# Converted weights: sign by a leaky slope on ScalarE, first loads on one queue, two maxima by GpSimd's queue

## The chip, the cores and the metric

One core of one Trainium2 chip. The metric is the device time of one execution in microseconds (us); lower is better. Before the change three runs gave a median of 1084.42 us (1084.20 to 1084.54).

## What is computed

A windowed attention whose weights are a softmax over seven taps, followed by a SiLU MLP. Cut from the reference (`x`: 4 x 4096 x 192, eight heads of 24 columns, `w_in`: 192 x 2048, `w_out`: 2048 x 192):

```python
w = softmax(weight_gen, axis=-1)                      # (B, S, 8 heads, 7 taps)
out[b, s, h, :] = sum_k w[b, s, h, k] * x_pad[b, s + k, h, :]   # window of 7, padded in front
h = out.reshape(16384, 192) @ w_in
result = (h * sigmoid(h)) @ w_out                     # (16384, 192), float32
```

`x` and `weight_gen` come as float32, `w_in` and `w_out` as float64. The chip gets each float64 as two 32-bit integers, low and high, and makes float32 of them itself.

## The kernel before, in words

**Tiling.** The 16384 rows lie 128 to a partition. They are worked in 32 blocks `b` of 512 rows (four per partition), each against 16 slices `f` of 128 hidden columns, taken as 8 pairs `p` (slices `p` and `p + 8`). For each pair (`b`, `p`) TensorE does `mm1` (the hidden columns, L497 for block 0, L509 from block 1), ScalarE the SiLU (`act`, L519 or L521 and L522), VectorE the low half of a two-part float16 split (`lower`, L527, from block 1), and TensorE the second product (`mm2_whole`, L550 and L554, or `mm2`, L541). Block 0 runs in float32 on the converted weights as they are. From block 1 on everything is split in two float16 parts, which needs a power of two as scale: one for each weight matrix, one for each chunk of `x`. Chunk 1 is block 1, chunk 2 is blocks 2 and 3, and the later chunks have four blocks each. `mm1` runs three pairs ahead of the second product, with four PSUM tiles for `h`, so two pairs of `h` can be open.

**Opening.** The engines' orders are written out by hand up to the end of block 1. First come the loads; then the softmax of block 0 (`top`, `sub`, `exp`, `tot`, `rec`, `norm`: L318 to L337); then seven products of `x` with a tap's weight on VectorE (L450), which TensorE sums in PSUM through an identity matrix (`total`, L455; the last two products are added on VectorE first, L460); copies to SBUF (L465, L466); a turn by TensorE (L471) with copies (L472); then `mm1` of block 0 (L497). 64 small matmuls at the start (L619) warm TensorE up.

**Weights.** Eight pieces of each matrix, `I0` to `I7` and `O0` to `O7`, are loaded as raw integers into nine buffers by SP's queue (L193, L196). Each piece is converted (`convert_steps`): `move` on ScalarE (L211) scales the high word, read as a float32, by 2^-112; `sign` on VectorE shifts the low word right (L173) and puts the high word's sign bit over it (L216); `join` (L220) shifts the moved value left by three and merges. `size` on ScalarE (L225) sums the absolute values of a piece, and of these sums the scale comes: `w_rows` (L254) on VectorE, a turn on TensorE (L257), a maximum on VectorE (L260), a spread over the partitions on TensorE (L264), and the scale on VectorE (`w_scale`). Then each piece is split (`upper_w` L238, `lower_w` L242).

**Scales of x.** For chunk 1 ScalarE sums absolute values (L640, `xs1`), TensorE turns the column into a row (L647), VectorE takes the maximum (L660), TensorE spreads it (L661). For chunk 2 (L666, `xs2`) and the later chunks the column goes by DMA to DRAM and back, spread over all partitions (`absmax_by_dma`, L160 and L161), on SP's queue.

**Order.** `OPENING` has a row for each of the first 16 pairs, with three strings of step names: before the pair's `mm1`, after its `act`, and inside the second product that follows. `I S J B U L` with a digit are move, sign, join, size, upper and lower of a piece of `w_in`; `O G Q D P R` the same of `w_out`; `n1`, `n2` the rest of the softmax of chunks 1 and 2; `M`, `A` products and sums of block 1's attention; `X` its split and transposes (L393, L396, L403, L388); `Wr Wa Wb Wc` the steps of the weight scale; `y` chunk 1's scale; `x2` the size of chunk 2 and its DMAs; `z2` chunk 2's scale from them; `g` the lower part of the pair before. Every engine and queue works in its order; a step that waits holds all behind it.

The lines that the diff touches, with those that call them:

Of the kernel before, what the change touches and what calls it, by code (L numbers as in the profile page):

```python
# [62 lines left out]
REBIAS = 2.0 ** -112  # L63
RAW = 9
SIGN = -0x80000000
# [4 lines left out]
def kernel(  # L70
# [132 lines left out]
    wsum = const.tile([P, 2, NP], F32, name="wsum")  # L203

    def convert_steps(kind, p):

        v, t = value(kind, p), stage.tile([P, 2 * D], I32, tag="t", name=f"t{kind}{p}", bufs=2)
        col = "IO".index(kind)

        def move():  # L210
            nc.scalar.activation(out=v, in_=raws[kind, p][..., 1].bitcast(F32), func=AF.Copy, scale=REBIAS)  # L211

        def sign():
            low, high = raws[kind, p][..., 0], raws[kind, p][..., 1]
# [8 lines left out]
        def size():
            junk = sm_p.tile([P, 2 * D], mybir.dt.bfloat16, tag="junk", name=f"junk{kind}{p}", bufs=1)
            nc.scalar.activation(out=junk, in_=v, func=AF.Abs, accum_out=wsum[:, col, p:p + 1])  # L225

        return [move, sign, join, size]
# [46 lines left out]
    def load_x(c):  # L274
# [4 lines left out]
        if t0 == 0:  # L279
# [5 lines left out]
            nc.scalar.dma_start(out=t[1:1 + cut, 0:HALO, :], in_=xf[0:cut, T - HALO:T, :])  # L285
            nc.scalar.dma_start(out=t[1 + cut:P, 0:HALO, :], in_=xf[cut:P - 1, T - HALO:T, :])
# [312 lines left out]
    with tc.manual_schedule():  # L599
        load_w(0)  # L600
        load_x(0)
        load_w(1, nc.scalar)
        load_w(2, nc.scalar)
# [5 lines left out]
        load_x(1)  # L609
        load_piece("I", 1)  # L610
# [19 lines left out]
        for f in (top1, sub1, exp1, step.pop("zeros"), top2, sub2, exp2):  # L630
            f()
        nc.scalar.activation(out=warm[:, 1:2], in_=ones[0:1, 0:1], func=AF.Silu)
        for k in range(5, 1, -1):
            mul(k)
            total(k, False, False)
        xs1 = sm_p.tile([P, 1], F32, tag="xs1", name="xs1", bufs=1)
        xs2 = sm_p.tile([P, 1], F32, tag="xs2", name="xs2", bufs=1)
        rows1 = (HALO + TB) * D
# [6 lines left out]
        px = ps_o.tile([P, 2, D], F32, tag="acc", name="x1_all").rearrange("p a d -> p (a d)")  # L645
        pw = ps_o.tile([P, 2, D], F32, tag="acc", name="w_all").rearrange("p a d -> p (a d)")
        nc.tensor.matmul(px[0:1, 0:P], xs1, ident, start=True, stop=True)  # L647
        total(1, False, True)

        conv = {(k, p): convert_steps(k, p) for k in "IO" for p in range(NP)}  # L650
        conv["I", 0][0]()
# [7 lines left out]
        x1r = sm_p.tile([1, 1], F32, tag="r", name="r_x1")  # L659
        nc.vector.tensor_reduce(out=x1r, in_=px[0:1, 0:P], op=ALU.max, axis=AX.X)  # L660
        nc.tensor.matmul(px[:, P:P + 1], ones[0:1], x1r, start=True, stop=True)  # L661

        def x2_size():
            n = (HALO + chunks[2][1]) * D
            junk = xv.rearrange("p t g n -> p (t g n)").bitcast(mybir.dt.bfloat16)[:, 0:n]
            nc.scalar.activation(out=junk, in_=x_t[2][:, 0:HALO + chunks[2][1], :].rearrange("p t d -> p (t d)"),  # L666
                                 func=AF.Abs, accum_out=xs2)
            got, (rows, over) = absmax_by_dma(xs2, "x2")
            rows()
            step["z2"] = lambda: (over(), x_scales(got, 2), finish_scales(2), out_scale(2))  # L670
# [149 lines left out]
```

## Time and profile before

| | |
|---|---|
| median of three runs | 1084.42 us |
| the profiled execution | 1084.3 us, of which its span is 1082.5 us |
| TensorE (PE) busy | 1049.9 us, 97% of the span |
| VectorE (DVE) busy | 784.7 us, 72% |
| ScalarE (ACT) busy | 775.0 us, 72% |
| GpSimd (POOL) busy | 293.2 us, 27% |
| DMA queue of SP / of ACT | 64.43 MB / 0.93 MB |

The span is what the profiler's records cover; 1.8 us lie around it. PE is the engine whose order fills the span; what it does not fill lies almost all in the first 100 us. Rows of the timeline give the start of a group of like instructions, the time to the end of its last one, the engine and line, output and input, shapes, and the count; in brackets stands the time that the engine sat idle before, and what ended it. SPq and ACTq are the issues of those engines' DMA queues.

### The profile page before, as it was taken

To read this page: it belongs to the slowest core of one execution; us is meant where nothing else is said; L and a number is where in the kernel's file an instruction comes from. 1 tells how busy PE (TensorE), PEld (TensorE's weight loads), DVE (VectorE), ACT (ScalarE), POOL (GpSimd) and SP (SyncE) were. 2 spreads that over 40 slices of the span, in tenths; PEclk is the share of its full clock that TensorE was granted. 3 is DMA by queue.
4 is the path that set the end of the run, shared out by engine and by line. 5 is a ranking of instruction groups with operands and counts; after the bars stand their busy time and mean duration, and the time that the engine had idled before them with its cause. 6 is when DMAs were issued, how large, how long until landed. Compare 5 with 4: busy or idle time off the path is not lost.

```text
span 1082.5 us, 36860 instructions
## 1 busy us (share of the span) xinstructions
PE 1049.9 (97%) x16472; PEld 811.3 (75%) x16472; DVE 784.7 (72%) x1134; ACT 775.0 (72%) x1264; POOL 293.2 (27%) x169
## 2 busy tenths in 40 slices
PE   6988999999999999999999998999999999999998
PEld 4655677777777777777777776777777777777776
DVE  6888886678866697677867686667886669767643
ACT  3765777678777777777767785767877777777775
POOL 1000343331513343312433304333151334331100
PEclk9999999999999999999999999999999999999999
DMA  8412132111411115111331104111131111211110
GB/s 214 139 30 118 42 133 50 39 45 32 131 46 45 39 38 145 32 31 46 91 85 46 46 19 142 39 39 46 31 131 46 45 38 40 48 31 32 45 46 16
DMA packets 73790, 67.71 MB, mean 63 GB/s; under 512 B 52639, under 2 KB 67103, under 8 KB 72606
## 3 DMA queue, kind: packets, MB, share of 16 engines
q1 hardware_dynamic: 73184, 64.43, 21.8%
q8 instruction: 128, 2.10, 0.9%
q10 hardware_dynamic: 446, 0.93, 0.3%
q14 instruction: 32, 0.26, 0.1%
HBM read 28.37 MB, written 12.59 MB: 38 GB/s over the span
## 4 chain that ended last, share of the span: by engine, by line
PE 77%; DVE 9%; ACT 6%; DMA 5%; issue 3%; SPq 0%; DVEq 0%; ACTq 0%
PE h L509 37%; PE acc L541 37%; DVE pr L424 2%; ACT h L521 2%; DVE g L527 1%; PE acc L554 1%; DVE pr L418 1%; DMA xc<-in_x_dram 1%; DMA xu<-xt 1%; DMA xt<-xs 1%; DVE xm L351 1%; ACT g L522 1%; DMA d_x<-xs 1%; PE sum L455 1%; PE h L497 1%
## 5 line engine op out<-in xcount | busy, mean ns | idle before, releaser
L527 DVE SCALAR_TENSOR_TENSOR g<-h,gup,g 128x512 f16<-128x512 f32 x496 | 369.0, 747 | 264.8 <-ACT g L522 264.4
L541 PE MATMUL acc<-wo,g 64*128 64x192 f16 x11424 | 556.6, 243 | 0.0
L541 PEld LDWEIGHTS <-g 64*128 64x128 f16 x11424 | 528.5, 94 | 25.2 <-issue 0.2
L521 ACT ACTIVATE h<-h,inv 128x512 f32<-128x512 f32 x496 | 326.5, 658 | 251.0 <-PE h L509 250.2
L509 PEld LDWEIGHTS <-w 64*128 64x128 f16 x4464 | 278.7, 94 | 203.4 <-issue 24.0
L522 ACT ACTIVATE g<-h,gup 128x512 f16<-128x512 f32 x496 | 341.0, 687 | 16.2
L509 PE MATMUL h<-xt,w 64*128 64x512 f16 x2232 | 310.7, 376 | 10.8 <-DVE g L527 10.8
L509 PE MATMUL h<-xu,w 64*128 64x512 f16 x2232 | 308.8, 377 | 4.3 <-DMA xu<-xt 4.3
L418 POOL TENSOR_TENSOR pr<-xc,wc 128x768 f32<-128x768 f32 x87 | 144.4, 1674 | 507.5 <-DVE pr L424 407.2
L418 DVE TENSOR_TENSOR pr<-xc,wc 128x768 f32<-128x768 f32 x130 | 130.9, 1008 | 0.0
L424 DVE TENSOR_TENSOR pr<-pr,pr 128x768 f32<-128x768 f32 x128 | 130.1, 1016 | 0.3
L424 POOL TENSOR_TENSOR pr<-pr,pr 128x768 f32<-128x768 f32 x58 | 122.2, 2107 | 4.5
L575 DVE SCALAR_TENSOR_TENSOR o<-acc,od,t 128x192 f32<-128x192 f32 x120 | 44.1, 408 | 3.5 <-ACT t L574 3.5
L574 ACT ACTIVATE t<-acc,od 128x192 f32<-128x192 f32 x120 | 43.6, 418 | 3.8 <-PE acc L554 3.8
L321 POOL TENSOR_TENSOR wc<-wc,wm 128x896 f32<-128x896 f32 x7 | 12.3, 1757 | 107.6 <-DVE wm L318 107.6
L396 DVE SCALAR_TENSOR_TENSOR xs<-pr,xup,xs 128x768 f16<-128x768 f32 x31 | 35.3, 1138 | 6.4 <-ACT xs L393 4.3
L337 POOL TENSOR_TENSOR wc<-wc,ws 128x896 f32<-128x896 f32 x7 | 12.3, 1754 | 89.6 <-DVE ws L334 89.6
L393 ACT ACTIVATE xs<-pr,xup 128x768 f16<-128x768 f32 x31 | 28.7, 925 | 9.1 <-DVE pr L424 9.1
L351 DVE TENSOR_REDUCE xm<-xc 128x1 f32<-128x960 f32 (+1 forms) x28 | 34.4, 1228 | 0.0
L550 PEld LDWEIGHTS acc<-v_out,g 128*128 128x128 f32 x128 | 21.4, 196 | 4.9 <-issue 1.8
L550 PE MATMUL acc<-v_out,g 128*128 128x192 f32 x128 | 24.3, 344 | 0.0
L554 PEld LDWEIGHTS <-g 128*128 128x128 f16 x240 | 20.1, 100 | 5.4 <-issue 5.1
(87 smaller groups left out, 254.6 us busy)
## 6 DMA issues: line engine op xcount, KB each, us to landing
xc<-in_x_dram SPq DMA_DIRECT2D x7, 2112.0 KB, 10.4
xu<-xt SPq DMA_DIRECT2D x62, 192.0 KB, 2.8
out_dram<-o SPq DMA_DIRECT2D x58, 192.0 KB, 1.9
wc<-in_weight_gen_dram SPq DMA_DIRECT2D x7, 448.0 KB, 6.4
rawI<-in_moe_w_in_dram SPq DMA_DIRECT2D x16, 192.0 KB, 6.5
rawO<-in_moe_w_out_dram SPq DMA_DIRECT2D x8, 384.0 KB, 4.3
xc<-in_x_dram SPq DMA_DIRECT2D x1, 1344.0 KB
xc<-in_x_dram SPq DMA_DIRECT2D x2, 384.0 KB, 6.0
```

The source lines that it names most:

```text
L351: nc.vector.tensor_reduce(out=m[:, i:i + 1], in_=x_t[c][:, cuts[i]:cuts[i + 1], :].rearrange("p t d -> p (t d)"), op=ALU.max, axis=AX.X, a ...
L396: nc.vector.scalar_tensor_tensor(out=xs[:, ts, D:2 * D], in0=acc, scalar=sc[c, "up"], in1=xs[:, ts, 0:D], op0=ALU.mult, op1=ALU.subtract)
L418: eng.tensor_tensor(out=pr[k].rearrange("p t (h g) -> p (t h) g", g=G), in0=xin, in1=wv, op=ALU.mult)
L424: eng.tensor_tensor(out=pr[k], in0=pr[k], in1=pr[l], op=ALU.add)
L509: nc.tensor.matmul(h_t[b, p + NP * i], w16[rows, g, part, p * P:(p + 1) * P], x_in[rows, :, k, :], start=n == 0, stop=n == NT9 - 1)
L521: nc.scalar.activation(out=h, in_=h, func=AF.Silu, scale=sc[c, "inv"])
L522: nc.scalar.activation(out=gh, in_=h, func=AF.Copy, scale=sc[c, "gup"])
L527: nc.vector.scalar_tensor_tensor(out=gl_t[b, f], in0=h, scalar=sc[chunk_of[b], "gup"], in1=gh_t[b, f], op0=ALU.mult, op1=ALU.subtract)
L541: nc.tensor.matmul(acc_t[b, i, t // 2][:, t % 2, :], g[rows, t * P:(t + 1) * P], wo16[rows, f, part], start=f == ORDER[0] and t % 2 == 0 a ...
L550: nc.tensor.matmul(acc_t[b, 0, t // 2][:, t % 2, :], gh_t[b, f][:, t * P:(t + 1) * P], v_out[:, f % NP, f // NP], start=f == 0 and t % 2 = ...
L574: nc.scalar.activation(out=t1, in_=a[0], func=AF.Copy, scale=sc[c, "od"])
L575: nc.vector.scalar_tensor_tensor(out=o[:, t, :], in0=a[1], scalar=sc[c, "od"], in1=t1, op0=ALU.mult, op1=ALU.add)
```

## The change

Five things are edited. `move` uses a leaky function: a positive value is scaled by 2^-112 as before, a negative one also by -2^32, which sets the bit that `join` shifts into the sign, so the merge of the sign bit on VectorE (L216) is gone and `rest` is the shift alone. `size` takes two pieces at once. The halo rows of `x` and the softmax weights of chunks 1 and 2 are loaded on SP's queue, where ACT's queue had them. The maxima of chunks 1 and 2 go through DRAM on GpSimd's queue; chunk 1's no longer passes TensorE. The order of the opening is written anew: the softmax starts of chunks 1 and 2 stand between products of block 0, and in `OPENING` six of `M` and `A` are ahead of `Wr`, `Wa` is half a second product later, and `z2` three pairs later.

```diff
-    ("", "D6 D7 Wr M3 A3", "Wa M2 A2"),
-    ("Wb M1 A1 M0 A0 X", "Wc U0 L0 U1 U2 P0 L1", "L2 U3 R0 P1 L3"),
+    ("", "D3 M1 A1 Wr M0 A0 X", ""),
+    ("Wa", "Wb", "Wc U0 U1 P0 L0 L1"),
...
-    wsum = const.tile([P, 2, NP], F32, name="wsum")
+    wsum = const.tile([P, 2, NP // 2], F32, name="wsum")
...
         def move():
-            nc.scalar.activation(out=v, in_=raws[kind, p][..., 1].bitcast(F32), func=AF.Copy, scale=REBIAS)
-
-        def sign():
-            low, high = raws[kind, p][..., 0], raws[kind, p][..., 1]
-            bits(t, low, 29, ALU.logical_shift_right)
-            nc.vector.scalar_tensor_tensor(out=t, in0=high, scalar=SIGN, in1=t,
-                                           op0=ALU.bitwise_and, op1=ALU.bitwise_or)
+            nc.scalar.activation(out=v, in_=raws[kind, p][..., 1].bitcast(F32), func=AF.Prelu, scale=REBIAS,
+                                 alpha=TO_BIT_31)
+
+        def rest():
+            bits(t, raws[kind, p][..., 0], 29, ALU.logical_shift_right)
...
-            nc.scalar.dma_start(out=t[1:1 + cut, 0:HALO, :], in_=xf[0:cut, T - HALO:T, :])
-            nc.scalar.dma_start(out=t[1 + cut:P, 0:HALO, :], in_=xf[cut:P - 1, T - HALO:T, :])
+            nc.sync.dma_start(out=t[1:1 + cut, 0:HALO, :], in_=xf[0:cut, T - HALO:T, :])
+            nc.sync.dma_start(out=t[1 + cut:P, 0:HALO, :], in_=xf[cut:P - 1, T - HALO:T, :])
...
-        load_w(1, nc.scalar)
-        load_w(2, nc.scalar)
+        load_w(1)
...
         load_x(1)
+        load_w(2)
...
-        for f in (top1, sub1, exp1, step.pop("zeros"), top2, sub2, exp2):
-            f()
-        nc.scalar.activation(out=warm[:, 1:2], in_=ones[0:1, 0:1], func=AF.Silu)
+        step.pop("zeros")()
+        between = {5: (top1, sub1, exp1), 4: (top2, sub2, exp2)}
         for k in range(5, 1, -1):
             mul(k)
             total(k, False, False)
+            for f in between.get(k, ()):
+                f()
+        nc.scalar.activation(out=warm[:, 1:2], in_=ones[0:1, 0:1], func=AF.Silu)
...
-        px = ps_o.tile([P, 2, D], F32, tag="acc", name="x1_all").rearrange("p a d -> p (a d)")
+        got1, (to_all1, over1) = absmax_by_dma(xs1, "x1", nc.gpsimd)
+        to_all1()
...
-        nc.tensor.matmul(px[0:1, 0:P], xs1, ident, start=True, stop=True)
+        spare = ps_o.tile([P, 2, D], F32, tag="acc", name="spare").rearrange("p a d -> p (a d)")
+        nc.tensor.matmul(spare[:, 0:P], ident16, ident16, start=True, stop=True)
...
-        x1r = sm_p.tile([1, 1], F32, tag="r", name="r_x1")
-        nc.vector.tensor_reduce(out=x1r, in_=px[0:1, 0:P], op=ALU.max, axis=AX.X)
-        nc.tensor.matmul(px[:, P:P + 1], ones[0:1], x1r, start=True, stop=True)
...
-            got, (rows, over) = absmax_by_dma(xs2, "x2")
+            got, (rows, over) = absmax_by_dma(xs2, "x2", nc.gpsimd)
```

**SP's queue, the first loads.** `wc` are the softmax weights, `xc` the rows of `x`, `raw` the pieces of the weights. Before:

```order
L307 DMA wc_112<-in_weight_gen_dram 128x224
L284 DMA xc_114<-in_x_dram 128x768
L193 DMA rawI_133<-in_moe_w_in_dram 64x3x256 x2
L299 DMA xc_114<-in_x_dram 128x768
L193 DMA rawI_137<-in_moe_w_in_dram 64x3x256 x2
```

After:

```order
L308 DMA wc_112<-in_weight_gen_dram 128x224
L285 DMA xc_114<-in_x_dram 128x768
L286 DMA xc_114<-in_x_dram 112x1152
L287 DMA xc_114<-in_x_dram 15x1152
L308 DMA wc_119<-in_weight_gen_dram 128x224
L193 DMA rawI_131<-in_moe_w_in_dram 64x3x256 x2
L300 DMA xc_114<-in_x_dram 128x768
L308 DMA wc_135<-in_weight_gen_dram 128x448
```

The two halo loads and both later softmax weights, four issues that stood first on ACT, now stand among SP's, and the first raw piece is behind them.

**VectorE, from the last pieces of the weights to the weight scale.** `pr` are products of block 1's attention (the first line number of a pair a product, the second a sum), `tI` and `tO` the scratch of a conversion. Before:

```order
L418 TENSOR_TENSOR pr_1_351<-xc_114,wc_119 128x768
L424 TENSOR_TENSOR pr_0_350<-pr_0_350,pr_1_351 128x768
L173 TENSOR_SCALAR tI_304<-rawI_165 128x384
L216 SCALAR_TENSOR_TENSOR tI_304<-rawI_165,tI_304 128x384
L220 SCALAR_TENSOR_TENSOR v_in<-v_in,tI_304 128x384
L173 TENSOR_SCALAR tO_311<-rawO_170 128x384
L216 SCALAR_TENSOR_TENSOR tO_311<-rawO_170,tO_311 128x384
L220 SCALAR_TENSOR_TENSOR v_out<-v_out,tO_311 128x384
...
L418 TENSOR_TENSOR pr_2_352<-xc_114,wc_119 128x768
L424 TENSOR_TENSOR pr_0_350<-pr_0_350,pr_2_352 128x768
L254 TENSOR_REDUCE w_rows<-wsum 128x2
```

After:

```order
L419 TENSOR_TENSOR pr_3_353<-xc_114,wc_119 128x768
L425 TENSOR_TENSOR pr_0_350<-pr_0_350,pr_3_353 128x768
L173 TENSOR_SCALAR tI_295<-rawI_165 128x384
L218 SCALAR_TENSOR_TENSOR v_in<-v_in,tI_295 128x384
L173 TENSOR_SCALAR tO_302<-rawO_170 128x384
L218 SCALAR_TENSOR_TENSOR v_out<-v_out,tO_302 128x384
...
L419 TENSOR_TENSOR pr_4_354<-xc_114,wc_119 128x768
L425 TENSOR_TENSOR pr_0_350<-pr_0_350,pr_4_354 128x768
L419 TENSOR_TENSOR pr_5_355<-xc_114,wc_119 128x768
L425 TENSOR_TENSOR pr_0_350<-pr_0_350,pr_5_355 128x768
L255 TENSOR_REDUCE w_rows<-wsum 128x2
```

A piece takes two instructions where it took three, and ahead of the reduction stand six products and five sums where three and two stood.

**GpSimd, its first work after the identity matrices.** `d_x` is the column in DRAM, `mb_x` its copy over all partitions. After (before, the memset was followed at once by the first product):

```order
L292 MEMSET xc_114 1x1152
L160 DMA d_x_309<-xs_286 128x1
L161 DMA mb_x_310<-d_x_309 128x128
L160 DMA d_x_660<-xs_287 128x1
L161 DMA mb_x_661<-d_x_660 128x128
L419 TENSOR_TENSOR pr_0_640<-xc_389,wc_135 128x768
```

Four DMAs stand ahead of the first product of block 3, each waiting for the size or the DMA before it.

## Rows read from the trace of the kernel before

**Rows 1.** The page: span, and busy time of TensorE with its weight loads.

```profile
span 1082.5 us, 36860 instructions
PE 1049.9 (97%) x16472; PEld 811.3 (75%) x16472; DVE 784.7 (72%) x1134; ACT 775.0 (72%) x1264; POOL 293.2 (27%) x169
```

**Rows 2.** Timeline of TensorE, sums of block 0 to block 1.

```profile
22.23 1.56 PE L455 MATMUL sum<-pr,ident 128*128 128x384 f32 x4
...
26.20 0.38 PE L661 MATMUL x_all<-r_x,ones 1*128 1x1 f32 x2 [0.84 <-DVE r_x L660]
26.51 8.01 PE L497 MATMUL h<-xv,v_in 64*128 64x256 f32 x48
34.45 2.87 PE L550 MATMUL acc<-v_out,g 128*128 128x192 f32 x16
...
56.34 0.38 PE L257 MATMUL w_all<-ident,w_rows 128*2 128x128 f32 x2 [3.60 <-DVE w_rows L254]
...
73.56 1.24 PE L509 MATMUL h<-xu,w 64*128 64x512 f16 x9 [1.07 <-DMA xu<-xt]
...
89.35 0.37 PE L509 MATMUL h<-xt,w 64*128 64x512 f16 x1 [2.60 <-DVE g L527]
```

**Rows 3.** Three stretches: busy time by engine, granted clock, DMA share, GB/s.

```profile
15.00:22.00 7.00, 7.00 (x17) 3.72 (x18) 6.50 (x9) 3.28 (x5) 0.00 (x0) 0.76 1.12 269
56.30:62.90 6.60, 6.56 (x25) 3.90 (x25) 6.46 (x9) 0.00 (x0) 0.00 (x0) 0.74 0.00 0
86.80:97.80 11.00, 8.17 (x61) 4.57 (x60) 10.22 (x19) 3.97 (x7) 0.00 (x0) 0.84 0.62 260
```

**Rows 4.** Timeline of all engines, loads to the last product of block 0.

```profile
5.48 0.39 DVE L318 TENSOR_REDUCE wm<-wc 128x32 f32<-128x224 f32 x1 [4.49 <-DMA wc<-in_weight_gen_dram]
...
6.26 1.28 ACT L623 ACT_TABLE_LOAD   x1 [6.26 <-DMA xc<-in_x_dram]
...
7.66 0.37 ACT L325 ACTIVATE wc<-wc 128x224 f32<-128x224 f32 x1
...
9.51 0.96 DVE L450 TENSOR_TENSOR pr<-xc,wc 128x768 f32<-128x768 f32 x1
...
19.19 0.96 DVE L460 TENSOR_TENSOR pr<-pr,pr 128x768 f32<-128x768 f32 x1
```

**Rows 5.** Timeline of VectorE, conversions to the weight scale.

```profile
26.07 0.34 DVE L173 TENSOR_SCALAR tI<-rawI 128x384 int32<-128x384 int32 x1
...
30.95 0.56 DVE L220 SCALAR_TENSOR_TENSOR v_out<-v_out,tO 128x384 int32<-128x384 int32 x1 [0.89 <-ACT v_out L211]
...
47.96 0.95 DVE L418 TENSOR_TENSOR pr<-xc,wc 128x768 f32<-128x768 f32 x1
...
49.82 0.35 DVE L173 TENSOR_SCALAR tI<-rawI 128x384 int32<-128x384 int32 x1
50.21 0.56 DVE L216 SCALAR_TENSOR_TENSOR tI<-rawI,tI 128x384 int32<-128x384 int32 x1
50.87 0.56 DVE L220 SCALAR_TENSOR_TENSOR v_in<-v_in,tI 128x384 int32<-128x384 int32 x1
...
51.34 0.35 DVE L173 TENSOR_SCALAR tO<-rawO 128x384 int32<-128x384 int32 x1
...
56.12 0.16 DVE L254 TENSOR_REDUCE w_rows<-wsum 128x2 f32<-128x16 f32 x1
```

**Rows 6.** Timeline of VectorE, block 1: split, chunk 2's scale, next lower pair.

```profile
65.16 1.02 DVE L396 SCALAR_TENSOR_TENSOR xs<-pr,xup,xs 128x768 f16<-128x768 f32 x1 [1.00 <-ACT xs L393]
...
87.41 0.28 DVE L166 TENSOR_REDUCE ra_x<-mb_x 128x1 f32<-128x128 f32 x1 [1.11 <-DMA mb_x<-d_x]
...
88.56 1.40 DVE L527 SCALAR_TENSOR_TENSOR g<-h,gup,g 128x512 f16<-128x512 f32 x2
```

**Rows 7.** The DMAs through DRAM (column out, and back), issue to landing.

```profile
DMA to landing us min/median/max: 4.0/5.1/9.0
```

**Rows 8.** Waits of TensorE over the whole span: total us, times, longest.

```profile
PE h L509 <- DMA xu<-xt: 4.3, 3, 2.8
```

More of the change, by code (lines that the diff above doesn't have):

```diff
@@ L63 @@
 REBIAS = 2.0 ** -112
+TO_BIT_31 = -2.0 ** 32
 RAW = 9
-SIGN = -0x80000000
 EXPONENT = 0x7F800000
@@ L221, in join, with size_w @@
                                            op0=ALU.logical_shift_left, op1=ALU.bitwise_or)
[L223 to L227, printed above, removed]
+        return [move, rest, join]
+    def size_w(kind, q):
+        v = v_in if kind == "I" else v_out
+        v = v[:, 2 * q:2 * q + 2].rearrange("p q a n -> p (q a n)")
+        col = "IO".index(kind)
+        junk = sm_p.tile([P, 4 * D], mybir.dt.bfloat16, tag="junk", name=f"junk{kind}{q}", bufs=1)
+        nc.scalar.activation(out=junk, in_=v, func=AF.Abs, accum_out=wsum[:, col, q:q + 1])
     def halves_of(kind, p):
@@ L635 @@
             total(k, False, False)
+            for f in between.get(k, ()):
+                f()
+        nc.scalar.activation(out=warm[:, 1:2], in_=ones[0:1, 0:1], func=AF.Silu)
         xs1 = sm_p.tile([P, 1], F32, tag="xs1", name="xs1", bufs=1)
         xs2 = sm_p.tile([P, 1], F32, tag="xs2", name="xs2", bufs=1)
+        conv = {(k, p): convert_steps(k, p) for k in "IO" for p in range(NP)}
+        conv["I", 0][0]()
         rows1 = (HALO + TB) * D
@@ L644 @@
         both(1, 0)
-        px = ps_o.tile([P, 2, D], F32, tag="acc", name="x1_all").rearrange("p a d -> p (a d)")
+        got1, (to_all1, over1) = absmax_by_dma(xs1, "x1", nc.gpsimd)
+        to_all1()
         pw = ps_o.tile([P, 2, D], F32, tag="acc", name="w_all").rearrange("p a d -> p (a d)")
-        nc.tensor.matmul(px[0:1, 0:P], xs1, ident, start=True, stop=True)
+        spare = ps_o.tile([P, 2, D], F32, tag="acc", name="spare").rearrange("p a d -> p (a d)")
+        nc.tensor.matmul(spare[:, 0:P], ident16, ident16, start=True, stop=True)
         total(1, False, True)
-        conv = {(k, p): convert_steps(k, p) for k in "IO" for p in range(NP)}
-        conv["I", 0][0]()
         conv["I", 0][1]()
@@ L677, in w_scale @@
             out_scale(1)
-        step |= {"y": lambda: x_scales({"all": px[:, P:P + 1]}, 1), "x2": x2_size, "n2": lambda: (tot2(), rec2(), norm2()), "n1": lambda: (tot1(), rec1(), norm1()),
+        step |= {"y": lambda: (over1(), x_scales(got1, 1)), "x2": x2_size, "n2": lambda: (tot2(), rec2(), norm2()), "n1": lambda: (tot1(), rec1(), norm1()),
                  "Wr": w_rows, "Wa": w_turn, "Wb": w_over, "Wc": w_scale}
         for p in range(NP):
-            for kind, names in (("I", "ISJ" "B" "UL"), ("O", "OGQ" "D" "PR")):
+            for kind, names in (("I", "ISJUL"), ("O", "OGQPR")):
                 steps = conv[kind, p] + [lambda k=kind, p=p: upper_w(k, p), lambda k=kind, p=p: lower_w(k, p)]
                 step.update({f"{n}{p}": f for n, f in zip(names, steps)})
+                if p % 2 == 0:
+                    step["BD"["IO".index(kind)] + str(p // 2)] = lambda k=kind, p=p: size_w(k, p // 2)
         for n in ("I0", "S0", "J0"):
```

18 rows, old and new, of the table OPENING are left out of this document.

## The prediction

> **What bounds the kernel now.** I read the page first: TensorE is busy for 97% of the span [rows 1], so a microsecond counts only where TensorE's own order moves. Then the timeline of TensorE [rows 2]: the reader is to look for the brackets. Up to 26.51 us it does little but sum block 0; from there its order is nearly closed, but for four gaps: 3.60 us for the weight scale's row sums, 1.07 for the swapped rows, 2.60 for a lower part on VectorE, and 0.84 for the maximum that stands ahead of the first `mm1`. Then the granted clock [rows 3]: its mean is 0.76, 0.74 and 0.84 over three stretches. As the clock has two levels, 1.2 and 2.4 GHz, the time at the lower is twice the missing share: 7.0 x 0.24 x 2 = 3.4 us, 6.6 x 0.26 x 2 = 3.4, 11.0 x 0.16 x 2 = 3.5. Each lost half of that, 1.7 us, and each followed a stretch in which TensorE had idled (the 3.60 and the 2.60, and the pauses between early sums). Last the timelines of all engines and of VectorE [rows 4 to 6] for what ends those gaps. Behind 100 us the instructions stand as before, on TensorE in the same order; what the opening wins should stay won, and what follows is priced at nothing because its relative order is unchanged.
>
> **The start, to the first `mm1`.** ScalarE issues four loads before anything else, the last of which waits for an earlier DMA, so it idles 6.26 us before its table load, and the first `exp` starts at 7.66, although VectorE is done with `sub` at 5.48 + 2 x 0.39 and two short hops, about 6.30 [rows 4]. Without these issues `exp` waits for `sub` alone: -1.3 us. The cost is on SP's queue, where four issues are added, but the pieces behind them are first read at 17 us or later, so I price that at nothing. If that cover failed, the conversions would start late by the wait.
>
> The first load, 112 KB, took from its issue at 0.74 to about 5.44 because the halo of ACT's queue moved at the same time; now it is alone at the head of the queue. Not later than before (0), and not sooner than the 4.0 us of a tiny transfer through DRAM [rows 7], which gives 0.7: I take the 0.7, as nearly no data moves beside it. The first product then starts at 9.51 - 1.3 - 0.7 = 7.5. From there to the last sum on VectorE were 9.68 us [rows 4], of which 0.45 was waiting; 9.2 of work are left, in another order. The sum starts at 16.7 and ends 0.96 later, 17.7.
>
> TensorE began its own last sum only at 22.23, some 2.1 us after VectorE's end at 20.15, because it was summing at the lower clock [rows 2, 3]. Now its sums come between softmax steps of VectorE, spread out, each shorter than its spacing on average, and the pauses are at most about 1 us. So it starts its last sum at 17.8. From 22.23 to 26.51 were 4.28 us; the maximum's wait of 0.84 and the 0.31 of its matmul go, 3.1 are left. The first `mm1` starts at 20.9, and I allow 0.1 for the load of chunk 2's weights, which are read at about 12.0 and landed at 12.6 before: **21.0, or -5.5 us**. Bounds: 20.5, and 23.5 with the lower clock again (2.1 more) and no gain at the load.
>
> **Conversions and the weight scale.** A piece takes 51.34 - 49.82 = 1.52 us on VectorE; without the merge 0.39 + 0.47 = 0.86 are left (shift to next start, join to next start) [rows 5]. From the first shift of `I1` (26.07) to `w_rows` (56.12) were 30.05 us. Fifteen merges go: 15 x 0.64 = -9.6. Three products and three sums of block 1 come ahead, 49.82 - 47.96 = 1.86 a pair: +5.6. Chunk 1's scale has one more reduction, +0.3. And since VectorE reaches the join of `O0` sooner, its 0.89 us wait for ScalarE grows to about 1.75, +0.9: ScalarE moves `O0` after the first SiLU, which TensorE times. Sum 27.2. VectorE starts these at 0.5 behind the first `mm1`, 21.5, and ends at 48.8. TensorE did 52.74 - 26.51 = 26.2 us of work up to its gap, and now half a second product more, 1.4, ahead of the turn [rows 2]: it arrives at 48.6. The gap is about 0.5 instead of 3.60, **-3.1**, and with no such idle time the clock stays, **-1.7**. Bounds of the gap: 0, and 3 if the pieces land late. ScalarE's move is one instruction as before, of the same tile; no row shows the leaky function, so I bound it by the 0.34 to 0.56 of VectorE's steps on the same tile and by twice the latter; the first is the likelier, and either lies in the shadow of VectorE. The sizes are halved in number, which helps ScalarE alone.
>
> Behind the turn the split waits for VectorE's last product and sum, 1.86, ScalarE's half, about 1.0, and its own 1.02 [rows 5, 6]: it ends at 52.7. It ended at 66.18, and the swapped rows came at 73.56, 7.4 later [rows 2, 6]: now 60.1. TensorE gets to them after two more pairs of products, about 61.6, so the 1.07 goes: **-1.1**.
>
> **Block 1.** The 2.60 us gap at 89.35 ends with a lower part that stood behind chunk 2's scale. That scale waited 1.11 us for its DMA and took 88.56 - 87.41 = 1.15 more [rows 6]. Three pairs later, without a wait, it leaves the gap at 2.60 - 2.26 = 0.3, and its own 1.15 comes where VectorE has slack of about the same: I leave 0.4 in all, **-2.2**, and the clock stays there too, **-1.7**. Bounds of the two: 0 and -4.3.
>
> **GpSimd's queue.** The two columns start about 18 and 63 us and are read at about 40 and 86: 22 us of cover each. On SP's queue two DMAs through DRAM took up to 9.0 + 5.1 = 14 us [rows 7]; chunk 2's also no longer stands ahead of a 2 MB load on SP. So I price them at nothing. The Trainium skill, page "SBUF — State Buffer", in its part on DMAs of the GpSimd queue ("The 'DVE blocks DMA' trap"), says otherwise: GpSimd writes their descriptors itself and is locked out while VectorE runs in its two-port mode; one of 620 ns took 3100 beside a copy. By its figure four DMAs would be about 10 us longer, an estimate from that page, and the sum would not change, as two of them stay inside each cover. No row here shows such a DMA.
>
> **The sum.** -5.5 - 3.1 - 1.7 - 1.1 - 2.2 - 1.7 = -15.3. The profiled execution took 1084.3 us (its span 1082.5 and 1.8 around it), within 0.1 of the median: **1069.0 us**.
>
> **The rivals.**
> *Half the covers fail.* TensorE's early sums are spread out, and in the trace such spreading preceded a fall of the clock; and VectorE and TensorE meet at the turn, at the spread and at each lower part within 1 us, so one late link stalls. For it: [rows 3]. Against: the pauses are shorter. Price: 2.1 at the sums, or 2.5 at the turn with 1.7 for the clock, or both: 1071.5 to 1077, about 1074.
> *Chunk 1's scale is late.* VectorE meets it in order at about 40 us, ahead of the last pieces and `w_rows`; each us beyond its 22 of cover is a us at the turn, plus 1.7 once the gap lasts. A chain of 30 us gives 8 + 1.7: about 1078. For it: the skill's rule, if descriptors starve for a run of VectorE's instructions and not one. Against: 14 us by rows.
> *Slower.* The same mechanism, decided at the point where the chain outlasts 22 us of cover and the 15.3 won, less the clock's 1.7: from about 35 us on. At 40 us the time is 1084.3 - 15.3 + 18 + 1.7 = 1089. Against: more than twice the slowest row.
> *The change wins nothing.* If what follows were bound by the loads of block 2 or by VectorE, the early start would be given back by 120 us. Then 1084. Against: TensorE has 97% of the span, and the work of block 2 is tied to TensorE's pairs, so it moves along.
>
> **How the numbers follow.** A measurement of this kernel can tell about 0.2%, 2.2 us, from no change. Forecast (1066 to 1071.5): 0.62. Covers half gone (1071.5 to 1077): 0.24. Late scale (1074 to 1082): 0.08. Nothing won: 0.03. Slower: 0.03. The likeliest gives 1069.0. The range reaches down to all gaps closed and every bound at its best, 5.5 + 0.5 + 3.6 + 1.7 + 1.1 + 2.6 + 1.7 = 16.7, so 1067.6, and to most of the 4.3 - 1.1 = 3.2 us that TensorE waits twice more for swapped rows behind 100 us [rows 8], as those landings depend on the transfers beside them: 1065.5. It reaches up to where covers fail, 1076. Faster 0.94, same 0.03, slower 0.03.
>
> **What would show it.** Right: the first L498 near 21 us, ScalarE's table load near 1 us; one instruction less a piece on VectorE; a wait at `w_rows` under 1.5 us; no wait for the swapped rows; the clock full from 15 to 100 us; `mb_x` landed by 35 and 80 us. Wrong: a clock of 0.5 during the sums, VectorE waiting for `mb_x` or for raw pieces, ScalarE's move over 0.6 us, or a new wait of TensorE behind 100 us as long as what was won.

## The result and the profile after

The changed kernel took 1069.23 us (median of 4 runs, 1067.54 to 1071.55), the kernel before 1084.31 beside it: ratio 0.9869, 95% interval 0.9841 to 0.9897. The forecast was 1069.0. Two later sets of four runs of the same kernel gave medians of 1068.68 and 1067.61. The profiled execution took 1067.54 us, 16.8 less than that of before; it is the fastest of its four, so the trace shows a little more won than the median.

The page after, its span and the busy time of TensorE:

```profile
span 1065.4 us, 36826 instructions
PE 1043.4 (98%) x16469; PEld 809.3 (76%) x16469; DVE 776.1 (73%) x1118; ACT 772.4 (72%) x1248; POOL 295.5 (28%) x173
```

TensorE is shorter by 6.5 us of busy time and the span by 17.1: most of what went was idle time, the rest matmuls at the lower clock. Windows of the first 100 us, before and after (columns as in [rows 3]):

```profile
0.00:100.00 100.00, 83.41 (x508) 55.10 (x510) 79.94 (x151) 58.26 (x119) 3.18 (x10) 0.95 0.47 134
0.00:100.00 100.00, 93.06 (x646) 62.63 (x647) 82.77 (x148) 65.42 (x116) 13.62 (x18) 1.00 0.59 143
```

Of the 32.6 us that TensorE stood idle before, 16.6 lay there, which is half and not "almost all", as the text ahead of the prediction has it. Now 6.9 us lie there, of 22.0. TensorE's timeline, to be laid beside [rows 2]:

```profile
8.96 6.97 PE L456 MATMUL sum<-pr,ident 128*128 128x384 f32 x20
...
16.68 1.56 PE L456 MATMUL sum<-pr,ident 128*128 128x384 f32 x4 [0.69 <-DVE pr L461]
...
19.89 8.01 PE L498 MATMUL h<-xv,v_in 64*128 64x256 f32 x48
...
42.45 3.32 PE L498 MATMUL h<-xv,v_in 64*128 64x512 f32 x12 [0.60 <-ACT g L520]
...
50.95 0.38 PE L258 MATMUL w_all<-ident,w_rows 128*2 128x128 f32 x2 [2.38 <-DVE w_rows L255]
...
62.92 1.25 PE L510 MATMUL h<-xt,w 64*128 64x512 f16 x9
63.79 1.24 PE L510 MATMUL h<-xu,w 64*128 64x512 f16 x9
...
76.75 1.25 PE L510 MATMUL h<-xt,w 64*128 64x512 f16 x9
...
80.88 1.25 PE L510 MATMUL h<-xt,w 64*128 64x512 f16 x9
```

The brackets at the swapped rows (63.79) and at the fourth pair of block 1 (76.75, which stood at 89.35) are gone. The one at `w_rows` is not: 2.38 us, where 0.5 was forecast. A new one stands at 42.45: 0.60 us for `act`, and behind it twelve matmuls in 3.32 us where they took 2.85 elsewhere. The granted clock, for [rows 3]:

```profile
15.00:22.00 7.00, 6.22 (x40) 4.37 (x40) 5.50 (x12) 4.35 (x8) 0.71 (x1) 1.00 1.12 267
48.00:56.00 8.00, 5.62 (x29) 3.16 (x28) 6.15 (x10) 4.67 (x10) 0.00 (x0) 1.00 0.00 0
56.00:63.00 7.00, 7.00 (x38) 4.85 (x40) 6.51 (x18) 5.93 (x12) 0.00 (x0) 1.00 0.76 192
87.00:98.00 11.00, 10.71 (x110) 7.62 (x108) 10.04 (x18) 7.82 (x12) 6.09 (x3) 1.00 0.30 62
```

All three falls of the clock are gone; it stands at the upper level throughout (1.00 in the row of the first 100 us). How much earlier TensorE was at each landmark, beside the forecast's terms summed up to there:

| landmark on TensorE | before, us | after, us | earlier by | forecast |
|---|---|---|---|---|
| first `mm1` of block 0 | 26.51 | 19.89 | 6.6 | 5.5 |
| first `mm1` of block 1 | 71.24 | 62.92 | 8.3 | 10.3 |
| its swapped rows | 73.56 | 63.79 | 9.8 | 11.4 |
| fourth pair of block 1 | 89.35 | 76.75 | 12.6 | 13.6 |
| fifth pair of block 1 | 95.75 | 80.88 | 14.9 | 15.3 |
| end of the span | 1082.5 | 1065.4 | 17.1 | 15.3 |

The sum holds within 0.4 us at the end of the opening, but not term by term: more was won at the start, and less from there to block 1. The last 2.2 us come behind the edited opening: before, a wait of 2.83 us for swapped rows at 660 us was followed by a stretch at clock 0.91; after, a wait of its kind came at 135 us and no fall followed. What stands at these two places is shown behind the experiments.

```profile
660.63 1.84 PE L509 MATMUL h<-xu,w 64*128 64x512 f16 x9 [2.83 <-DMA xu<-xt]
```

```profile
135.38 1.24 PE L510 MATMUL h<-xu,w 64*128 64x512 f16 x9 [2.08 <-DMA xu<-xt]
```

Where did `w_rows` lose its 2 us, and TensorE the time at 42.45? The pieces reached the engines late. Timeline of ScalarE and of GpSimd in the changed kernel:

```profile
31.71 0.57 ACT L211 ACTIVATE v_out<-rawO 128x384 f32<-128x384 f32 x1 [4.22 <-DMA rawO<-in_moe_w_out_dram]
...
35.13 0.57 ACT L211 ACTIVATE v_out<-rawO 128x384 f32<-128x384 f32 x1 [1.45 <-DMA rawO<-in_moe_w_out_dram]
...
38.67 0.56 ACT L211 ACTIVATE v_out<-rawO 128x384 f32<-128x384 f32 x1 [2.97 <-DMA rawO<-in_moe_w_out_dram]
```

```profile
16.81 0.71 POOL L160 DMA_DIRECT2D d_x<-xs  x1 [8.72 <-ACT v_out L645]
31.81 0.56 POOL L161 DMA_DIRECT2D mb_x<-d_x  x1 [14.28 <-DMA d_x<-xs]
```

and its windows (the last two columns are the DMA share and GB/s):

```profile
24.00:28.00 4.00, 4.00 (x21) 1.80 (x18) 3.32 (x8) 3.49 (x8) 0.00 (x0) 1.00 1.43 27
28.00:32.00 4.00, 4.00 (x22) 3.10 (x24) 2.90 (x8) 0.29 (x1) 0.19 (x1) 1.00 0.50 39
32.00:36.00 4.00, 4.00 (x24) 2.96 (x20) 3.62 (x7) 2.25 (x5) 0.36 (x1) 1.00 1.01 246
```

From 24 to 32 us the loads ran at 27 to 39 GB/s, with pieces issued and waited for. They picked up when the column of chunk 1, 128 values of 4 bytes, had landed in DRAM (its read-back is issued at 31.81 us). Issue to landing of that column was 14.7 us, as much as both DMAs of such a chain took at most before (14, [rows 7]). The column's own packets are not what filled these 8 us: 32 of them stand between 22.3 and 23.1 us, 3.3% of the engines' time there, beside loads that still ran, and none from 24 to 30 us. The slow stretch lies between them and the landing. Between 24 and 30 us only 179 packets of loads moved, and they took 117.5% of 16 engines for 6 us: 1.175 x 96 / 179 = 0.63 us each.

```profile
q1 hardware_dynamic: 179, 0.18, 117.5%
```

The first question for the experiments is whether that column did it.

### The profile page after: what moved, and what is told of

It reads as the page before. It is cut to its first block, busy times and chain, and to the rows that moved or that the text cites. A ratio compares the mean times of both kernels' runs of the same rounds, so it can differ in the third digit from the quotient of the medians.

```text
span 1065.4 us, 36826 instructions
## 1 busy us (share of the span) xinstructions
PE 1043.4 (98%) x16469; PEld 809.3 (76%) x16469; DVE 776.1 (73%) x1118; ACT 772.4 (72%) x1248; POOL 295.5 (28%) x173
## 4 chain that ended last, share of the span: by engine, by line
PE 78%; DVE 9%; ACT 6%; issue 3%; DMA 3%; SPq 0%; DVEq 0%; ACTq 0%
PE h L510 38%; PE acc L542 38%; DVE g L528 2%; DVE pr L425 2%; ACT h L522 2%; DVE pr L419 1%; DMA rawO<-in_moe_w_out_dram 1%; PE acc L555 1%; ACT g L523 1%; PE h L498 1%; DVE xm L352 1%; ACT L522 1%; ACT L326 1%; DMA xu<-xt 1%; DVE wm L319 1%
## 5 line engine op out<-in xcount | busy, mean ns | idle before, releaser
L498 PE MATMUL h<-xv,v_in 64*128 64x512 f32 (+1 forms) x108 | 22.7, 553 | 0.7 <-ACT g L520 0.6
```

## The experiments

Twelve runs follow, two of them of the changed kernel itself. They were made in three batches, each on a chip of its own beside the kernel before (medians 1083.34, 1082.09 and 1082.51). A run is the median of four executions, if no other number is given.

**First group: the column.** The changed kernel again:

> The changed kernel once more. If the trickle of the DMA engines from 24 to 32 us (3 to 60 GB/s with pieces of the weights waiting) is part of the change, it is there again in the same place, O3 lands 14 us after its issue, and TensorE waits 2 to 3 us at w_rows. If it was a single disturbance, the pieces land by 28 us and the wait is under 1 us. Time 1067 to 1072 us either way.

1068.68 us (1066.57 to 1070.54), ratio 0.9863 (0.9841 to 0.9884). The slow stretch is there again, milder: the loads ran at 52 to 144 GB/s from 24 to 32 us and the column landed after 13.6 us. The wait for `w_rows` was 4.27 us, longer than expected; behind it TensorE's matmuls ran at the lower clock, as the second row shows against 2.85 us after the shorter wait:

```profile
52.30 0.38 PE L258 MATMUL w_all<-ident,w_rows 128*2 128x128 f32 x2 [4.27 <-DVE w_rows L255]
52.61 4.54 PE L498 MATMUL h<-xv,v_in 64*128 64x512 f32 x12
```

Run e1_px takes chunk 1's maximum through TensorE, as before, and leaves the rest of the change:

```
- got1, (to_all1, over1) = absmax_by_dma(xs1, "x1", nc.gpsimd)
- to_all1()
+ nc.tensor.matmul(px[0:1, 0:P], xs1, ident, start=True, stop=True)
+ nc.vector.tensor_reduce(out=x1r, in_=px[0:1, 0:P], op=ALU.max, axis=AX.X)
+ nc.tensor.matmul(px[:, P:P + 1], ones[0:1], x1r, start=True, stop=True)
```

> Chunk 1's maximum through TensorE as before the change, all else as after. Theory W (the write of the column on GpSimd's queue holds up the loads behind it): no trickle from 24 to 32 us, O3 landed by 26 us, no wait of ScalarE for raw pieces, the wait at w_rows under 1 us; the first L498 starts 1.1 us later (21.0 us), so that the time is about 1 to 2 us below the changed kernel, 1067. Rival Q (the pieces come late because all loads stand on one queue and wait for buffers): the trickle stays, w_rows waits 2.4 us as before, and the time is 1.1 us above the changed kernel, 1070.

1066.43 us (1066.28 to 1067.77), ratio 0.9842 (0.9826 to 0.9859). No trickle, and the wait for `w_rows` is short. Windows of e1_px, its load packets from 24 to 30 us, and its row at `w_rows`:

```profile
24.00:28.00 4.00, 4.00 (x22) 1.88 (x20) 2.04 (x5) 3.81 (x9) 0.00 (x0) 1.00 0.79 200
28.00:32.00 4.00, 4.00 (x24) 2.81 (x20) 3.58 (x11) 3.44 (x9) 0.00 (x0) 1.00 0.98 296
```

```profile
q1 hardware_dynamic: 1136, 1.32, 84.7%
```

```profile
49.60 0.38 PE L258 MATMUL w_all<-ident,w_rows 128*2 128x128 f32 x2 [0.78 <-DVE w_rows L255]
```

A packet of the loads took 0.847 x 96 / 1136 = 0.07 us, against 0.63. So the column held up the loads, on another queue, and not only itself. The time is 2.2 us below the repeat of the change, but the ranges of the two overlap. Run e2_hw_write leaves the column where the change has it, but writes it from ScalarE's queue:

```
- queue.dma_start(out=d.unsqueeze(1), in_=m1)
+ (out or queue).dma_start(out=d.unsqueeze(1), in_=m1)
```

> Chunk 1's column is written by a DMA issued from ScalarE's queue, and read back on GpSimd's. Theory W1 (it is GpSimd's queue that holds the loads up): the write lands within 10 us of its issue and the loads run at over 200 GB/s to the end; w_rows waits under 1 us, first L498 about 0.5 us later; time 1067. Theory W2 (it is the write of 128 times 4 bytes to DRAM that holds them up, from whatever queue): trickle of 5 to 8 us again, w_rows waits 2 to 3 us; time 1070.

1066.49 us (1065.81 to 1067.44). The column took 10.3 us, where it took 12.6 to 14.7 in the three profiles of the change; the loads ran at 49 and 81 GB/s in the two windows from 24 to 32 us and were back to speed some 2 us sooner, though the wait for `w_rows` was 2.37 us as in the change. That is theory W2 in all but its time: the trickle goes with the write, whichever queue issues it, and from GpSimd's queue the write lands later. The time is as low as that of e1_px, which had neither trickle nor wait, so these medians do not show what the wait costs in the end. Run e3_more_writes adds two more such writes:

```
+ for i in range(2):
+     more = dr_p.tile([P], F32, tag=f"more{i}", name=f"more{i}", bufs=1)
+     nc.gpsimd.dma_start(out=more.unsqueeze(1), in_=xs1)
```

> Two more writes of the same column to DRAM on GpSimd's queue ahead of the one that is used. Theory W: the trickle becomes longer, from 8 us to 16 or more, the last pieces land after 45 us, w_rows waits 8 us or more and the time rises to 1076 or more. Rival Q: the trickle stays at 8 us, and only GpSimd's own chain is 1.5 us longer, which has 5 us of cover; time as the changed kernel, 1069.

1072.21 us (1070.56 to 1073.59), ratio 0.9895 (0.9878 to 0.9913). Windows of e3_more_writes, and ScalarE's wait for a piece:

```profile
24.00:28.00 4.00, 4.00 (x20) 2.00 (x18) 2.64 (x7) 4.00 (x10) 0.00 (x0) 1.00 1.44 57
28.00:32.00 4.00, 4.00 (x24) 2.98 (x22) 3.29 (x9) 0.20 (x1) 0.00 (x0) 1.00 1.29 33
32.00:36.00 4.00, 4.00 (x23) 2.54 (x20) 0.00 (x0) 0.00 (x0) 0.00 (x0) 1.00 0.74 34
36.00:40.00 4.00, 1.52 (x9) 1.19 (x8) 1.39 (x3) 1.61 (x4) 0.55 (x1) 0.94 0.71 40
```

```profile
38.39 0.56 ACT L211 ACTIVATE v_out<-rawO 128x384 f32<-128x384 f32 x1 [10.19 <-DMA rawO<-in_moe_w_out_dram]
```

With two more writes of 128 times 4 bytes the trickle lasts 16 us instead of 8, and the last piece that is waited for lands at 45.9 us, as theory W said. Its wait and its time did not come: `w_rows` waited 0.92 us and not 8, and the time is 1072.2 and not 1076. TensorE had stood before, 2.48 and 2.63 us, for `act`, which comes behind the waiting moves in ScalarE's order. That the write causes the trickle is shown by these runs: without it there is none, from another queue it is there, with three it lasts twice as long. Why a write does this is not shown.

**Second group: the parts of the change.** Run e8_late is e1_px with the reduction and the spread of chunk 1's maximum moved behind the first conversions (steps `r1` and `s1` in `OPENING`), so that the first `mm1` doesn't wait for them.

> As the run with chunk 1's maximum through TensorE, but its row reduction and its spread stand later, where neither engine waits for the other: the reduction between two conversions, the spread ahead of the fourth mm1. Theory W: no trickle, no wait of 0.8 us at the spread, the first L498 at 20.2 us, the wait at w_rows about 1 us; 1065.3 us, 1.1 below the run with it ahead. Rival: the start won there is lost again at w_rows, because VectorE, not TensorE, sets that point: the same 1066.4.

1068.23 us (1067.28 to 1070.55), ratio 0.9872 (0.9849 to 0.9895). No trickle, 0.60 us at `w_rows`; but the halo landed late (VectorE's memset waited 1.18 us for it, 0.61 in the change), and the first `mm1` came at 21.50, not 20.2. The gain expected over e1_px was not seen. That late halo belongs to the execution: e9_sign and e11_z2, the same up to there, have the first `mm1` at 20.52 and 20.49. The next three undo one part each, from e8_late. Run e9_sign puts the merge of the sign back on VectorE:

```
- func=AF.Prelu, scale=REBIAS, alpha=TO_BIT_31)
+ func=AF.Copy, scale=REBIAS)
+ nc.vector.scalar_tensor_tensor(out=t, in0=high, scalar=-0x80000000, in1=t,
+                                op0=ALU.bitwise_and, op1=ALU.bitwise_or)
```

> As the run with the late spread, with the sign merged on VectorE again (copy on ScalarE, 16 more instructions on VectorE). Theory C (VectorE's instructions set w_rows): 15 x 0.64 = 9.6 us more on the way, the wait at w_rows 9 to 10 us, the clock at its lower level behind it for 1.7 more: 1076. Rival S (VectorE has slack on the way, ScalarE or the loads set w_rows): less than 3 us, 1068.

1076.09 us (1075.09 to 1076.63), 7.9 more than e8_late: theory C, with a wait a little shorter than it said. TensorE stands before `w_rows`, and the row behind the wait is at the lower clock (0.59 for 0.38):

```profile
56.60 0.59 PE L260 MATMUL w_all<-ident,w_rows 128*2 128x128 f32 x2 [8.24 <-DVE w_rows L257]
```

Run e10_actq puts the four loads back on ScalarE's queue:

```
- nc.sync.dma_start(out=t[1:1 + cut, 0:HALO, :], in_=xf[0:cut, T - HALO:T, :])
+ nc.scalar.dma_start(out=t[1:1 + cut, 0:HALO, :], in_=xf[0:cut, T - HALO:T, :])
...
- load_w(1)
+ load_w(1, nc.scalar)
+ load_w(2, nc.scalar)
```

> As the run with the late spread, with the halo and the softmax weights of chunks 1 and 2 on ScalarE's queue again. Theory L (the four issues keep ScalarE and slow the first load): the first load is used at 5.5 us, the first exp starts at 7.7, the first L498 4 us later, at 24 us; of that some 0 to 1 us is made up at w_rows: 1069. Rival: only the issues' place counts, the load lands as early as now, 1.5 us: 1066.8.

1069.28 us (1068.43 to 1070.2), 1.05 more than e8_late, which is within the spread of the two. The trace is plainer and is that of theory L: the first load is used at 5.32 us and ScalarE's table load stands at 6.63, near the two of [rows 4]; the first `mm1` starts at 24.02, 2.5 us later than in e8_late and 3.5 later than in e9_sign and e11_z2.

```profile
5.32 0.39 DVE L319 TENSOR_REDUCE wm<-wc 128x32 f32<-128x224 f32 x1 [4.32 <-DMA wc<-in_weight_gen_dram]
```

Run e11_z2 takes chunk 2's scale (`z2` in `OPENING`) three pairs earlier, to where it stood before:

> As the run with the late spread, with chunk 2's scale where it stood before the change, three pairs earlier, its DMAs on GpSimd's queue as now. Theory Z (its place counts, as its DMAs take 13 to 15 us): VectorE reaches it at 73 us and waits to 78, TensorE stands 4 to 5 us at the second pair's lower parts and then runs 1.7 us behind at the lower clock: 1071. Rival: TensorE's work stands far enough ahead, under 1 us: 1066.

1073.82 us (1073.12 to 1075.52), 5.6 more than e8_late: theory Z, with more lost than it said. The gap of [rows 2] is back, longer than it was (4.17 for 2.60), and the clock falls behind it: nine matmuls in 2.55 us, not 1.25.

```profile
78.98 2.55 PE L510 MATMUL h<-xt,w 64*128 64x512 f16 x9 [4.17 <-DVE g L528]
81.30 2.34 PE L510 MATMUL h<-xu,w 64*128 64x512 f16 x9
```

**Third group: the start, and what is left.** Run e7_loads_only is the kernel before with the first loads' queue and order of the change, and nothing else of it.

> The kernel before with the queue of the first loads alone changed: the halo and wm of chunks 1 and 2 on SP's queue, in the order of the change; sign merge, softmax order and both maxima as before. Theory of the sum: the first load is used at about 2.9 us (5.48 before) and the first L498 comes at 22.5 to 24 us (26.51); the pieces cost 1.52 us of VectorE as before, the waits for w_rows (3.60) and for g at 89.35 (2.60) stay within 1 us of what they were, and the time is 1079.5 to 1081.5 (before 1084.3). Rival: the conversion is bound by VectorE alone, so the earlier start goes into a longer wait for w_rows (over 6 us) and the time stays within 1 us of before.

1083.67 us (1079.85 to 1086.24, 10 runs), ratio 0.9998 (0.9981 to 1.0016): no difference. The sum fell; the rival has the time right and its reason wrong, as the wait for `w_rows` did not grow. The first load is used 2.6 us sooner, yet the first `mm1` comes at 27.92, later than the 26.51 of before; and the wait for `w_rows` is 3.61. Timelines of e7_loads_only, VectorE and TensorE, and its window of the sums:

```profile
2.91 0.39 DVE L318 TENSOR_REDUCE wm<-wc 128x32 f32<-128x224 f32 x1 [1.92 <-DMA wc<-in_weight_gen_dram]
...
8.88 0.39 DVE L318 TENSOR_REDUCE wm<-wc 128x32 f32<-128x224 f32 x1 [2.24 <-DMA wc<-in_weight_gen_dram]
...
13.03 0.62 DVE L318 TENSOR_REDUCE wm<-wc 128x64 f32<-128x448 f32 x1 [2.03 <-DMA wc<-in_weight_gen_dram]
```

```profile
15.23 8.17 PE L455 MATMUL sum<-pr,ident 128*128 128x384 f32 x16 [5.25 <-DVE pr L450]
```

```profile
15.00:22.00 7.00, 6.76 (x13) 3.81 (x14) 6.83 (x10) 3.64 (x5) 0.00 (x0) 0.59 1.12 245
```

VectorE now waits, in its order, for the weights of chunks 1 and 2, whose softmax starts stand ahead of six of block 0's products: 2.24 and 2.03 us, where before it waited 0 and 0.16. Those six products begin at 14.23 us, before at 13.87, however early the first one was; so TensorE idles 5.25 us between its sums (2.79 before) and then sums at a mean clock of 0.59 (0.76, [rows 3]). Run e12_softmax_first asks the same from the other side: e8_late with those softmax starts put back ahead of the products.

```
- between = {5: (top1, sub1, exp1), 4: (top2, sub2, exp2)}
+ for f in (top1, sub1, exp1, step.pop("zeros"), top2, sub2, exp2):
+     f()
+ between = {}
```

> Run e8_late with the maxima, subtractions and exponentials of chunks 1 and 2 put back ahead of chunk 0's first product, as in the kernel before. Theory: the first product is held up by what stands ahead of it (about 1.5 to 2 us of VectorE and ACT work), TensorE stands idle longer before its first sums, they run longer at a lower clock, and the first L498 comes 1.5 to 2.5 us later than in e8_late (21.50); the time is 1069.5 to 1071. Rival: the products and not their start set the first sums' end, so the first L498 moves by under 0.5 us, and the time stays at 1067 to 1068.5.

1070.52 us (1069.98 to 1073.06), ratio 0.9887 (0.9868 to 0.9905), 2.3 more than e8_late on another chip, in ranges that overlap. The first `mm1` starts at 25.63, 4.1 us later than in e8_late: the theory, with a larger step than it said.

```profile
14.40 7.77 PE L456 MATMUL sum<-pr,ident 128*128 128x384 f32 x16 [5.20 <-DVE pr L451]
```

So at the start the new queue alone wins nothing, and the new order alone little: in e10_actq the first `mm1` stands 2.5 us ahead of the kernel before, of which 0.84 and 0.31 belong to the maximum that left its place. Both together win 5.0 in e8_late and 6.0 in e11_z2, with the same share of the maximum in it. Last, run e13_halo_first tries for what is left: chunk 1's maximum through TensorE, late; the halo ahead of `x` on the queue; `Wr` ahead of one product and sum.

> The changed kernel with chunk 1's maximum taken through TensorE, its reduction and spread late in the conversion, the halo loads ahead of x0 on SP's queue, and w_rows ahead of M1 and A1. Theory: all that is left of the front's waits goes. The memset of xc on VectorE then waits under 0.3 us for the halo (0.6 in the profile of the change, 1.2 in run e8_late), the first L498 starts at 19.5 to 20.0 us (19.89 and 21.50), the loads keep over 150 GB/s from 24 to 32 us, TensorE waits under 0.3 us for w_rows (2.38 and 0.60), and the time is 1065.0 to 1066.5. Rival: what is left is set by the one wait of 2 to 3 us in the repeated part, which comes at another place in nearly every execution; the front then shows the same gains, and the time stays at 1067 to 1068.5, as in e8_late.

> The changed kernel unchanged, beside e13_halo_first. Theory: 1067.5 to 1070, with the loads at 20 to 60 GB/s while the column of chunk 1 is under way and a wait of 2 to 4.5 us for w_rows. Rival, that the trickle is a matter of single executions: over 150 GB/s from 24 to 32 us and a wait for w_rows under 1 us.

Side by side: e13_halo_first 1067.35 us (1066.88 to 1068.17), the changed kernel again 1067.61 (1066.3 to 1070.26). The first `mm1` of e13_halo_first came at 21.22 and not before 20: with the halo ahead, the first product waited 1.52 us for `x` (it starts at 7.08, not 5.63). No wait for `w_rows` was left, though 0.99 us now stood at the spread behind it. In r1_after_again the trickle stood again (49 to 87 GB/s from 24 to 32 us), with 2.5 us at `w_rows`. The rival is borne out: the times do not differ. The front does: the fifth pair of block 1 starts at 79.5, 79.9 and 80.0 us in e1_px, e8_late and e13_halo_first, and at 80.2 to 83.9 in the four profiles with the column (the change, its two repeats, e2_hw_write). What the front wins without the column is for the most part lost again behind it.

It is lost in a wait of TensorE for swapped rows, of 1.9 to 2.9 us, which stands once behind 120 us in twelve of the fourteen profiles, and not at all in those of e2_hw_write, the kernel with the lowest single time (1065.81 us), and of e3_more_writes. Its place goes with the kernel: near 135 us in the three profiles of the change, at 644 to 653 us in the seven runs that take chunk 1's maximum through TensorE, at 661 and 663 us in the kernel before and in e7_loads_only. At each of these places a column stands again, that of a later chunk, on SP's queue. Timeline of SP's queue in the changed kernel:

```profile
127.30 1.10 SPq L389 DMA_DIRECT2D xu<-xt  x2
128.49 0.54 SPq L160 DMA_DIRECT2D d_x<-m_x  x1
135.84 0.33 SPq L161 DMA_DIRECT2D mb_x<-d_x  x1
```

The two DMAs of swapped rows are issued right ahead of the column. One landed 2.7 us after its issue, as ever, the other after 7.5, where the median of such DMAs is 3.0; it landed half a microsecond ahead of the column, and TensorE went on at 135.38. In all twelve profiles the late DMA is one with a column right behind it. So the column of a later chunk is the likely cause of what is left too, but no run moved it, and in six of seven such places of a profile the swapped rows land in time. Why one of them does not is open.

In six of the twelve the matmuls behind the wait also ran slower (1.60 to 2.29 us for nine, not 1.24). The length of the wait does not decide that: they were slow behind 2.06 us in e13_halo_first and not behind 2.66 in e8_late. That this wait sets the spread of 2 to 4 us between runs of one kernel fits all this but was not tried by itself.

## Why the prediction was right, and where its steps were not

- **The start (-5.5, measured -6.6).** The mechanism was right, and one term was mis-sized. "Not sooner than the 4.0 us of a tiny transfer through DRAM" was a wrong floor: alone at the head of the queue, the 112 KB landed 2.2 us after issue, so the load gave 2.56 us and not 0.7. Part went back in waits for the halo (0.61 and 0.20 us), now behind `x` on the same queue. In the repeats the start was 6.0 and 6.2 us earlier. The split of the 5.5 into a load and an `exp` was also a wrong picture: e7_loads_only shows that the loads win nothing without the softmax order, and e12_softmax_first that the order is worth 4.1 us of the first `mm1` (from e8_late, whose halo was late).
- **Conversions (27.2 us from the first shift to `w_rows`, measured 50.74 - 20.32 = 30.4).** A piece took 27.59 - 26.65 = 0.94 us, not 0.86, in all 1.2 us more (rows below). The wait at `O0` was 1.77 (1.75 forecast), and ScalarE's leaky move took 0.54 to 0.58 us, inside its bounds and as long as the copy before. The rest is VectorE's waits for pieces, on their load or on ScalarE's late move of them: 0.85 + 0.24 + 1.20 + 0.23 = 2.5 us; the other steps took 0.5 less. That VectorE waits for raw pieces is one of the signs that the prediction named for being wrong.

```profile
26.65 0.35 DVE L173 TENSOR_SCALAR tI<-rawI 128x384 int32<-128x384 int32 x1
27.11 0.56 DVE L218 SCALAR_TENSOR_TENSOR v_in<-v_in,tI 128x384 int32<-128x384 int32 x1
27.59 0.35 DVE L173 TENSOR_SCALAR tI<-rawI 128x384 int32<-128x384 int32 x1
```

- **The gap at `w_rows` (0.5, measured 2.38).** This is the step that failed: "So I price them at nothing" of GpSimd's queue. TensorE arrived at 48.57, as forecast (48.6); VectorE's reduction stood at 50.74 (48.8). The cover of 22 us held, but not for the reason given: the two DMAs took 14.7 and 7.0 us with the issue of the second between them, 22 and not 14, and the value landed at about 38.8 us (the sign said 35) and was read at 41.60 without a wait. What was not priced was what the column does to others: it slowed the loads of the pieces, so the cover of the loads failed through the column and not through their own order. It also cost what TensorE lost at 42.45, 0.60 and 0.47 us: the `act` that it waited for stands behind the move that waited until 38.67, and ScalarE had no pause between. The bound ("3 if the pieces land late") held the value here, and not the 4.27 of r0_again.
- **The clock (-1.7 twice, and 2.1 at the sums).** Right: no stretch of the opening is at the lower level. At `w_rows` it was near: it stayed after waits of 2.38 us (2.37 and 2.50 in other profiles) and fell after one of 4.27 (r0_again); the half-failed rival is what that execution shows at the turn.
- **Swapped rows (-1.1) and block 1 (-2.2, -1.7).** Right; no wait of over 0.3 us is left there, and e11_z2 shows that in block 1 the moved scale did it.
- **The rule on GpSimd's queue.** The Trainium skill, page "SBUF — State Buffer" ("SBUF: two separate sides", the callout "The 'DVE blocks DMA' trap"), says that a DMA of GpSimd's queue waits for its descriptors while VectorE runs an operation in its two-port mode. The column's 14.7 us against 10.3 from ScalarE's queue agree in direction, but that rule bears on the start of a transfer, and there they differ by 1.9 us: the first packets stand 5.5 us after the issue (22.3 - 16.81) against 3.6 (21.5 - 17.89). The larger part of the difference lies behind the packets, 8.4 against 4.0 us to the landing. By the Trainium skill, page "SBUF — State Buffer", in the same callout, a DMA of ScalarE's or SP's queue runs at full speed beside VectorE. Here the loads on SP's queue crawled, in e2_hw_write too, where the write was ScalarE's. The Trainium skill, page "DMA: Bandwidth & Descriptors" ("Specifications"), says that transfers under 512 bytes are done by reading, changing and writing back; the column is 128 of 4 bytes. That this is why it holds up others no run here shows.
- **The sum.** -15.3 against -14.9 at the end of the opening: +1.1 at the start, -3.1 from there to block 1 (1.9 at `w_rows`, 1.1 at 42.45), +1.6 in block 1. That the median came within 0.2 us of the forecast is so in part luck: these offset each other, and the runs of the kernel spread over 4 us. The undone parts (7.9, 2.3, 1.05, 5.6) add to 16.9 us, but e8_late lies 13.9 below before. They may overlap, a loss in front being taken up by a later wait, but two of the four are no larger than the spread of their runs.
- **What the maximum by GpSimd's queue brought.** For chunk 1, no run shows a gain: e1_px, without it, was 2.2 us faster than the repeat beside it and e13_halo_first 0.3 faster, in ranges that overlap, and e2_hw_write, with it, was as fast as e1_px. Up to 100 us it costs (the landmarks above); over the whole span that is not settled, as the later wait comes at another place.
- **What no run undid alone.** The sizes by two pieces, chunk 2's maximum on GpSimd's queue, the products ahead of `Wr` and the place of `Wa` were not tried by themselves (e13_halo_first moved `Wr` together with other things). Their share is argued only.

## What to carry to other kernels

A transfer is priced not only by its own wait but by what it does to transfers beside it: a column of 128 four-byte values written to DRAM doesn't belong among loads that are waited for. An earlier load only pays if the order of the engines lets the work behind it start, so try queue and order together. A gap on TensorE is to be counted with the slower matmuls behind it: a scale moved by three pairs, with no work saved, was worth 5.6 us. And what an opening wins is to be followed to the end of the span, as a later wait can take it back.

## What was not expected of the hardware

- One write of 512 bytes in 128 pieces held up loads on another queue for about 8 us (27 to 39 GB/s instead of 200 to 296, and 49 to 144 in two repeats; 0.63 us a packet instead of 0.07), issued by GpSimd's queue or, for some 6 us, by ScalarE's, and three such writes for 16 us. From GpSimd's queue the write's own packets were done within a microsecond, ahead of that stretch.
- A load of 112 KB took 2.2 us from issue to landing alone at the head of a queue, and 4.7 us when ScalarE's queue was given the halo and two more loads at the same time (4.5 in e10_actq).
- ScalarE's leaky function with a slope of -2^32 on the negative side cost no more than the plain copy (0.54 to 0.58 us on 128 x 384).
